# The low halves of the first MLP's weights, computed by GpSimd instead of VectorE

## The chip, the cores and the metric

The kernel runs on one core of a Trainium2 chip. The metric is the device time of one execution in microseconds, the median of the runs shown. The engines are TensorE (PE in the profile; its weight loads are PEld), VectorE (DVE), ScalarE (ACT), GpSimd (POOL) and SyncE (SP), which issues the transfers. Each works through its own instructions strictly in a fixed order, and semaphores hold an instruction until what it needs is there.

## The reference

An attention over windows of 32 queries, then two MLPs on its output, all in float32. The weights of the MLPs have their values in 8-byte cells when they come in, of which the kernel makes float32 again.

```python
def _attn_ref(q, k, v, mem_k, mem_v):            # q: 4 x 8 heads x 768 x 64
    for c in range(S // 32):                     # 16 keys of context left, 8 right, 8 memory keys
        k_full = np.concatenate([mem_k, k_ctx], axis=2)
        scores = scale * np.matmul(q_c, k_full.transpose(0, 1, 3, 2))
        a = softmax(scores)
        out[:, :, c_start:c_end] = np.matmul(a, v_full)

def _moe_ref(x, w_in, w_out):                    # x: 3072 x 512, w_in: 512 x 2048
    h = x @ w_in
    g = np.where(h > 0.0, h, np.exp(np.minimum(h, 0.0)) - 1.0)
    return g @ w_out

def _moe2_ref(x, w_in, w_out, s, b):             # same sizes
    r = np.maximum(x @ w_in, 0.0)
    return (s * (r * r) + b) @ w_out
```

## The kernel before

**Split matmuls.** TensorE multiplies in a reduced float32 format (F32R). To keep precision, each operand is split into a high half, the value rounded to that format, and a low half, the rest. A product is then three matmuls (`mm3`, L326 to L328): high by high, high weight by low data, low weight by high data. The third, L328, is the one that reads a weight's low half.

**The weights of the first MLP** are 32 slots: for each of 16 hidden chunks c, one slot of w_in (i = 0) and one of w_out (i = 1), 128 x 512 each. `load_w` (L125) brings a slot's 8-byte cells into a tile `raw`. `to_f32` takes them apart: two ScalarE conversions (L131, L132) and two VectorE merges (L135, L138) that leave the float32 value in a tile `t`, of which there are three buffers in turn (pool `wst`). Then `split_w` makes the halves: ScalarE writes the high one (L149), and L150 subtracts it from the value. In the profile L150's instruction stands at L184, the line of the helper `sub`, with the tile name w. `raw` and the finished pair share a place in memory, and every slot has a place of its own.

**The work beside it.** The attention goes by 24 units of 128 queries, each with scores (L219, psS or psVS), a softmax on VectorE and ScalarE (L228 to L237), transposes of the probabilities into `pt` (by TensorE, L251, for units 0 to 5; from unit 6 on by VectorE, L258) and values (L278, psV or psVS). From unit 6 on, one unit's values and the next one's scores share a pair of PSUM banks (`step_VS`). The tokens are 8 tiles of 384, three units each. For a tile t and a chunk c, `h1` does 12 matmuls into a bank psH (two such banks in turn, which the transposes of units 0 to 5 use too), then ScalarE (L350, L351) and VectorE (L352) make g in one buffer, and `split_g` its halves gh (ScalarE, L180) and gl (VectorE, L184). `out1` does 12 matmuls into four accumulators, two chunks behind `h1`. The sequence is tile 0 with chunks 0 to 5, tile 1 with all 16, tile 0 with the rest, then tiles 2 to 7. So each weight is made just before its first use for chunks 0 to 5 of tile 0, and some chunks ahead of it in tile 1. The second MLP follows with its own preparation, on which the change doesn't bear.

**What sets the order.** The program is written as steps in an order of priority (`weights_to` hands out weight steps beside attention and MLP steps); a scheduler then puts the instructions of each engine into one fixed row, by its own estimate of when each could start. A change of one instruction's engine can therefore move others.

Of the kernel before, what the change touches and what calls it, by code (L numbers as in the profile page):

```python
# [13 lines left out]
ALU = mybir.AluOpType  # L14
# [39 lines left out]
def tile_attention_then_two_mlps(ctx, tc, q_in, k_in, v_in, w1, w2, s_in, b_in, out):  # L54
# [17 lines left out]
    nc = tc.nc  # L72
# [43 lines left out]
    def f(t):  # L116
        return t.bitcast(F32)
# [10 lines left out]
    def to_f32(raw, t):  # L128

        low, high = raw[:, :, 0], raw[:, :, 1]  # L130
        nc.scalar.activation(out=f(high), in_=f(high), func=AF.Copy, scale=2.0 ** -112)  # L131
        nc.scalar.activation(out=low, in_=low.bitcast(U32), func=AF.Copy, scale=2.0 ** -29 * (1 - 2.0 ** -15),  # L132
                             bias=-0.4999)
        yield
        nc.vector.scalar_tensor_tensor(out=t, in0=high, scalar=3, in1=low,  # L135
                                       op0=ALU.logical_shift_left, op1=ALU.bitwise_or)
        yield
        nc.vector.scalar_tensor_tensor(out=t, in0=high, scalar=-0x80000000, in1=t,  # L138
                                       op0=ALU.bitwise_and, op1=ALU.bitwise_or)
        yield  # L140

    def split_w(c, i, raw):

        t = wst.tile([P, DM], I32, tag="t", name="t")
        yield from to_f32(raw, t)
        nm = "io"[i]
        parts = wps[c >= NFREE].tile([P, 2, DM], F32R, tag=f"w{i}_{c}", name=f"w{i}_{c}")
        hi, lo = parts[:, 0], parts[:, 1]
        nc.scalar.activation(out=hi, in_=f(t), func=AF.Copy)  # L149
        sub(lo, f(t), hi)  # L150
        W[nm, c], WT[nm, c] = (hi, lo), parts
        yield

# [8 lines left out]
    op = [actx.enter_context(tc.tile_pool(name="op", bufs=3))]  # L162
# [20 lines left out]
    def sub(lo, src, hi):  # L183
        return nc.vector.tensor_tensor(out=lo, in0=src, in1=f(hi), op=ALU.subtract)  # L184
# [310 lines left out]
    def weights_to(w, n, ahead):  # L495

        while wnext[0] < min(n, MICRO * NF):
            k, m = divmod(wnext[0], MICRO // 2)
            c, i = divmod(k, 2)
            load_ws(w, k + 1 + ahead)  # L500
            if m == 0:
                wsteps[:] = [split_w(c, i, wraw[k])]
            next(wsteps[0])
            wnext[0] += 1
# [297 lines left out]
```

## Time and profile before

| | |
|---|---|
| Median of 3 runs | 1099.0 us (1098.36 to 1099.37) |
| The profiled execution, its own time | 1097.48 us |
| Its span, first to last instruction | 1095.7 us |
| TensorE busy | 1076.3 us (98%), 8206 matmuls |
| VectorE busy | 783.9 us (72%), 1299 instructions |
| ScalarE busy | 591.9 us (54%), 939 instructions |
| GpSimd busy | 0.7 us, 6 instructions |

Busy times are of the profiled execution. Matmuls overlap in the pipeline, so that one of 384 columns is shown 336 ns long while the next starts some 0.17 us after it; a busy TensorE may still lose time between two. VectorE's instructions overlap a little too. The first 120 us, in which the weights of the first MLP are made, are a small part of the span; the shares above don't describe them.

### The profile page before, as it was taken

How to read it: one execution, taken by the hardware profiler on the slowest of the kernel's cores; microseconds unless marked ns; L12 is line 12 of the kernel's file. 1: busy time of each engine (PE TensorE's matmuls, PEld its weight loads, DVE VectorE, ACT ScalarE, POOL GpSimd, SP SyncE). 2: the span in 40 equal slices, each digit the busy share in tenths (PEclk: the TensorE clock that was granted, in tenths of full speed). 3: DMA queues.
4: the chain of work that ended last, by engine and by line, in shares of the span. 5: the costliest groups of instructions: out<-in, count | busy, mean ns of one | idle time of the engine just before them, and what ended most of it. 6: DMA issues, size and time to landing. Idle time of an engine off the chain costs nothing.

```text
span 1095.7 us, 20629 instructions
## 1 busy us (share of the span) xinstructions
PE 1076.3 (98%) x8206; PEld 964.4 (88%) x8206; DVE 783.9 (72%) x1299; ACT 591.9 (54%) x939; POOL 0.7 (0%) x6
## 2 busy tenths in 40 slices
PE   7999999999999999999999999999999999999998
PEld 5889999999999999999999987788888788888886
DVE  6899856777777777898884656796266695375844
ACT  4888534344344346887875455644355653355542
POOL 0000000000000000000000000000000000000000
PEclk7999999999999999999999999999999999999999
DMA  8965032442433316888876366777767777776773
GB/s 305 377 223 214 1 109 94 146 144 93 142 117 121 114 40 206 328 329 303 328 289 253 90 192 190 240 211 224 229 192 196 222 207 226 207 193 192 205 190 124
DMA packets 98113, 213.70 MB, mean 195 GB/s; under 512 B 9952, under 2 KB 27360, under 8 KB 95968
## 3 DMA queue, kind: packets, MB, share of 16 engines
q1 hardware_dynamic: 97440, 211.59, 60.3%
q8 instruction: 65, 1.06, 0.4%
q10 hardware_dynamic: 576, 0.79, 0.2%
q14 instruction: 32, 0.26, 0.1%
HBM read 164.89 MB, written 47.45 MB: 194 GB/s over the span
## 4 chain that ended last, share of the span: by engine, by line
PE 87%; DVE 6%; DMA 4%; ACT 3%; issue 1%; SPq 0%; ACTq 0%; DVEq 0%
PE psH L326 14%; PE psH L328 14%; PE psH L327 14%; PE psL L327 7%; PE psL L328 7%; PE acc L326 7%; PE psL L326 7%; PE acc L327 7%; PE acc L328 7%; DVE pt L258 2%; DMA xc<-y_dram 1%; PE psVS L278 1%; DMA xl<-x_dram 1%; PE psVS L219 1%; PE psV L278 1%
## 5 line engine op out<-in xcount | busy, mean ns | idle before, releaser
L326 PE MATMUL psH<-xh,w 128*128 128x384 f32 x512 | 174.9, 342 | 2.4 <-ACT pt L180 1.0
L326 PE MATMUL acc<-gh,w 128*128 128x384 f32 x512 | 172.7, 338 | 1.3 <-DVE big L380 0.8
L328 PE MATMUL psH<-xh,w 128*128 128x384 f32 x512 | 173.0, 338 | 0.0
L327 PE MATMUL psH<-xl,w 128*128 128x384 f32 x512 | 172.6, 337 | 0.2 <-DVE xl L184 0.2
L328 PE MATMUL acc<-gh,w 128*128 128x384 f32 x512 | 171.8, 336 | 0.0
L327 PE MATMUL acc<-gl,w 128*128 128x384 f32 x512 | 171.7, 335 | 0.0
L702 ACT ACTIVATE g2h<-g 128x1024 fp32r<-128x1024 f32 x84 | 88.9, 1058 | 95.6 <-PE psL L328 95.5
L327 PE MATMUL psL<-g2l,ws 128*128 128x512 f32 x336 | 133.0, 396 | 1.4 <-DVE g2l L184 1.4
L184 DVE TENSOR_TENSOR g2l<-g,g2h 128x1024 fp32r<-128x1024 f32 x84 | 102.3, 1222 | 44.3 <-ACT g2h L702 44.0
L328 PE MATMUL psL<-g2h,ws 128*128 128x512 f32 x336 | 132.9, 395 | 0.0
L326 PE MATMUL psL<-g2h,ws 128*128 128x512 f32 x336 | 132.5, 396 | 0.1
L326 PE MATMUL psH<-xc,ws 128*128 128x512 f32 x336 | 131.7, 397 | 0.5 <-ACT p L653 0.5
L327 PE MATMUL psH<-xc,ws 128*128 128x512 f32 x336 | 131.0, 390 | 0.0
L328 PE MATMUL psH<-xc,ws 128*128 128x512 f32 x336 | 131.0, 390 | 0.0
L350 ACT ACTIVATE g<-psH 128x384 f32<-128x384 f32 x128 | 62.5, 488 | 111.9 <-PE psH L328 65.3
L180 ACT ACTIVATE gh<-g 128x384 fp32r<-128x384 f32 x128 | 67.0, 523 | 88.0 <-DVE g L352 86.9
L352 DVE SCALAR_TENSOR_TENSOR g<-g,psH 128x384 f32<-128x384 f32 x128 | 70.4, 550 | 47.8 <-ACT g L351 46.9
L326 PEld LDWEIGHTS psH<-xh,w 128*128 128x128 f32 x512 | 96.7, 189 | 5.1 <-ACT pt L180 1.2
L326 PEld LDWEIGHTS acc<-gh,w 128*128 128x128 f32 x512 | 96.1, 188 | 2.8 <-DVE big L380 1.1
L327 PEld LDWEIGHTS psH<-xl,w 128*128 128x128 f32 x512 | 96.7, 189 | 0.5 <-DVE xl L184 0.4
L328 PEld LDWEIGHTS psH<-xh,w 128*128 128x128 f32 x512 | 96.7, 189 | 0.2
L327 PEld LDWEIGHTS acc<-gl,w 128*128 128x128 f32 x512 | 96.2, 188 | 0.1
(97 smaller groups left out, 1667.9 us busy)
## 6 DMA issues: line engine op xcount, KB each, us to landing
ws<-s_dram SPq DMA_DIRECT2D x336, 256.0 KB, 3.0
raw<-w SPq DMA_DIRECT2D x64, 512.0 KB, 5.5
s_dram<-right SPq DMA_DIRECT2D x16, 1024.0 KB, 4.6
kb<-k SPq DMA_DIRECT2D x24, 512.0 KB, 5.5
v<-v SPq DMA_DIRECT2D x24, 512.0 KB, 4.1
s_dram<-left SPq DMA_DIRECT2D x16, 768.0 KB, 3.6
q<-q SPq DMA_DIRECT2D x24, 256.0 KB, 5.4
out<-r SPq DMA_DIRECT2D x24, 256.0 KB, 3.5
```

The source lines that it names most:

```text
L180: return nc.scalar.activation(out=hi, in_=src, func=AF.Copy)
L184: return nc.vector.tensor_tensor(out=lo, in0=src, in1=f(hi), op=ALU.subtract)
L219: mm = nc.tensor.matmul(ps[o, z, r * NCK:(r + 1) * NCK], q[rows, r * U + c * CH:r * U + (c + 1) * CH], kb[rows, r, c * NCK:(c + 1) * NCK], ...
L258: nc.vector.transpose(out=pt[k * CH:(k + 1) * CH, :, rows], in_=sm[rows, :, z, n0:n0 + CH])
L278: nc.tensor.matmul(ps[r % 2 * D:(r % 2 + 1) * D, z, o:o + CH], v[rows, (r * NC + c) * D:(r * NC + c + 1) * D], pt[rows, r, cs], start=True ...
L326: nc.tensor.matmul(o, sa(a[0]), sb(b[0]), start=first, stop=False, skip_group_check=again)
L327: nc.tensor.matmul(o, sa(a[0]), sb(b[1]), start=False, stop=False, skip_group_check=again)
L328: return nc.tensor.matmul(o, sa(a[1]), sb(b[0]), start=False, stop=last, skip_group_check=again)
L350: nc.scalar.activation(out=g[:, :n], in_=ps[:, :n], func=AF.Relu, scale=-1.0)
L352: nc.vector.scalar_tensor_tensor(out=g[:, :n], in0=g[:, :n], scalar=-1.0, in1=ps[:, :n], op0=ALU.add, op1=ALU.max)
L702: nc.scalar.activation(out=gh, in_=g[:, block], func=AF.Copy)
```

## The change

One line of `split_w`: the subtraction is issued to GpSimd, with the same operands and the same result. In the profile it then has its own line, L150. The 32 instructions wait for ScalarE's high half; the merges that reuse a buffer `t` wait for GpSimd.

```diff
@@ split_w
         hi, lo = parts[:, 0], parts[:, 1]
         nc.scalar.activation(out=hi, in_=f(t), func=AF.Copy)
-        sub(lo, f(t), hi)
+        nc.gpsimd.tensor_tensor(out=lo, in0=f(t), in1=f(hi), op=ALU.subtract)
         W[nm, c], WT[nm, c] = (hi, lo), parts
```

The scheduler's rows move with it. VectorE before, around the weights of chunks 4 and 5 (t is the value, raw_c the cells of a slot of chunk c, w_c its halves, sm the probabilities, nmx their maxima):

```order
L138 SCALAR_TENSOR_TENSOR t<-raw_4_653,t 128x512
L228 TENSOR_TENSOR sm_103<-psS,cmask_92 128x2x4x64
L138 SCALAR_TENSOR_TENSOR t<-raw_5_713,t 128x512
L184 TENSOR_TENSOR w_4_853<-t,w_4_853 128x512
L231 TENSOR_REDUCE nmx<-sm_103 128x8
L184 TENSOR_TENSOR w_5_925<-t,w_5_925 128x512
L232 TENSOR_TENSOR sm_103<-sm_103,nmx 128x2x4x64
L352 SCALAR_TENSOR_TENSOR g<-g,psH 128x384
```

The same place of VectorE now:

```order
L228 TENSOR_TENSOR sm_103<-psS,cmask_92 128x2x4x64
L138 SCALAR_TENSOR_TENSOR t<-raw_5_713,t 128x512
L231 TENSOR_REDUCE nmx<-sm_103 128x8
L135 SCALAR_TENSOR_TENSOR t<-raw_5_744 128x512
L232 TENSOR_TENSOR sm_103<-sm_103,nmx 128x2x4x64
L138 SCALAR_TENSOR_TENSOR t<-raw_5_744,t 128x512
L352 SCALAR_TENSOR_TENSOR g<-g,psH 128x384
```

The two subtractions are gone, and the merges of the next slot stand in their place.

TensorE before, where chunk 5 of tile 0 begins (w_5_925 is chunk 5 of w_in):

```order
L278 MATMUL psV<-pt,v 64x32 x10
L326 MATMUL psH<-xh,w_5_925 128x384
L327 MATMUL psH<-xl,w_5_925 128x384
L278 MATMUL psV<-pt,v 64x32 x16
L328 MATMUL psH<-xh,w_5_925 128x384
```

TensorE there now:

```order
L328 MATMUL acc_760<-gh,w_3_751 128x384
L326 MATMUL psH<-xh,w_5_925 128x384
L327 MATMUL psH<-xl,w_5_925 128x384
L328 MATMUL psH<-xh,w_5_925 128x384
L326 MATMUL psH<-xh,w_5_925 128x384
```

The value matmuls between the second and the third matmul of the chunk went behind the chunk. At chunk 3 it is the same; at chunks 2 and 4 a unit's 32 score matmuls now stand in that gap.

TensorE before, after the last chunk of tile 0's first part, where unit 6's values and unit 7's first scores stand (psVS):

```order
L328 MATMUL acc_761<-gh,w_5_956 128x384
L278 MATMUL psVS<-pt,v 64x32 x32
L219 MATMUL psVS<-kb,q 32x64 x7
L326 MATMUL psH<-xh,w_2_592 128x384
L327 MATMUL psH<-xl,w_2_592 128x384
```

TensorE now, at the place of unit 7's values, 366 rows later, when unit 6's step has come 48 matmuls earlier:

```order
L328 MATMUL psH<-xh,w_9_1264 128x384
L278 MATMUL psVS<-pt,v 64x32 x9
L326 MATMUL acc_1996<-gh,w_7_1131 128x384
L327 MATMUL acc_1996<-gl,w_7_1131 128x384
L278 MATMUL psVS<-pt,v 64x32 x3
L328 MATMUL acc_1996<-gh,w_7_1131 128x384
L278 MATMUL psVS<-pt,v 64x32
L326 MATMUL acc_1997<-gh,w_7_1131 128x384
L327 MATMUL acc_1997<-gl,w_7_1131 128x384
L278 MATMUL psVS<-pt,v 64x32 x19
```

Unit 6's step no longer stands among the first chunks of tile 1 but behind all of them, 48 matmuls of the MLP ahead of unit 7's; between unit 7's and unit 8's steps stand 54 more after these rows, where before there were 60.

## Rows read from the trace of the kernel before

**Rows 1.** Stretches in us: busy us (instructions) by engine, granted clock, DMA share, GB/s

```profile
core 0: us, PE busy (x) PEld busy (x) DVE busy (x) ACT busy (x) POOL busy (x), PEclk, DMA share, GB/s
10.00:34.20 24.20, 18.40 (x418) 15.22 (x416) 19.05 (x38) 13.91 (x25) 0.00 (x0) 0.65 0.90 337
34.20:72.40 38.20, 36.41 (x484) 32.37 (x484) 37.43 (x75) 35.67 (x69) 0.00 (x0) 1.00 0.74 288
72.40:81.40 9.00, 7.46 (x121) 6.13 (x119) 8.80 (x20) 7.34 (x15) 0.00 (x0) 1.00 0.79 259
...
100.00:121.00 21.00, 21.00 (x122) 21.00 (x121) 20.68 (x38) 14.15 (x28) 0.00 (x0) 1.00 0.06 14
121.00:160.00 39.00, 39.00 (x343) 38.62 (x342) 22.18 (x51) 15.87 (x31) 0.00 (x0) 1.00 0.25 77
```

**Rows 2.** Tile w, subtractions: ns min/median/max, first and last start; then 34.2 to 72.4

```profile
L184 DVE TENSOR_TENSOR w<-t,w x32: 679/684/694, 16.4 to 120.3; 128x512 fp32r<-128x512 f32 x32
...
L184 DVE TENSOR_TENSOR w<-t,w x11: 679/684/693, 38.0 to 70.1; 128x512 fp32r<-128x512 f32 x11
```

**Rows 3.** Order of time, VectorE, 57 to 61 us: start, busy us, what

```profile
57.35 0.68 DVE L184 TENSOR_TENSOR w<-t,w 128x512 fp32r<-128x512 f32 x1
57.95 0.68 DVE L231 TENSOR_REDUCE nmx<-sm 128x8 f32<-128x512 f32 x1
58.55 0.68 DVE L184 TENSOR_TENSOR w<-t,w 128x512 fp32r<-128x512 f32 x1
...
59.75 0.55 DVE L352 SCALAR_TENSOR_TENSOR g<-g,psH 128x384 f32<-128x384 f32 x1
60.21 0.69 DVE L135 SCALAR_TENSOR_TENSOR t<-raw 128x512 int32<-128x512 int32 x1
```

**Rows 4.** Groups of GpSimd: busy us, mean ns | idle before

```profile
masks.py:199 POOL TENSOR_SCALAR_AFFINE_SELECT ident<-ident 128x128 f32<-128x128 f32 x1 | 0.3, 292 | 0.1
masks.py:197 POOL MEMSET ident<- 128x128 f32 x1 | 0.2, 205 | 0.3 <-POOLq L785 0.3
...
L785 POOL MEMSET const-float32-0.0<- 128x1 f32 x1 | 0.1, 98 | 0.2 <-issue 0.2
```

**Rows 5.** Groups of g and its halves, 0 to 420 us, columns as in rows 4

```profile
L184 DVE TENSOR_TENSOR gl<-g,gh 128x384 fp32r<-128x384 f32 x80 | 44.4, 556 | 20.2 <-ACT gh L180 19.5
L352 DVE SCALAR_TENSOR_TENSOR g<-g,psH 128x384 f32<-128x384 f32 x80 | 44.0, 551 | 33.6 <-ACT g L351 32.9
...
L351 ACT ACTIVATE g<-g 128x384 f32<-128x384 f32 x80 | 42.0, 524 | 2.0
L350 ACT ACTIVATE g<-psH 128x384 f32<-128x384 f32 x81 | 39.7, 490 | 86.8 <-PE psH L328 55.1 <-DVE gl L184 30.8 <-PE acc L328 0.8
```

**Rows 6.** Order of time, ScalarE and TensorE, 57 to 60 us, start of chunk 5

```profile
57.65 0.63 ACT L149 ACTIVATE w<-t 128x512 fp32r<-128x512 f32 x1
...
58.89 0.67 PE L278 MATMUL psV<-pt,v 64*64 64x32 f32 x32
59.49 0.44 PE L328 MATMUL psH<-xh,w 128*128 128x384 f32 x1
```

**Rows 7.** Order of time, TensorE, 72 to 76 us, with idle time and releaser

```profile
72.51 0.95 PE L278 MATMUL psVS<-pt,v 64*64 64x32 f32 x24
...
75.06 0.78 PE L278 MATMUL psVS<-pt,v 64*64 64x32 f32 x38 [0.36 <-DVE pt L258]
75.76 0.34 PE L219 MATMUL psVS<-kb,q 64*32 64x64 f32 x14
```

**Rows 8.** Order of time, TensorE and VectorE, 151 to 166 us, units 7 and 8

```profile
151.37 1.14 PE L278 MATMUL psVS<-pt,v 64*64 64x32 f32 x64
152.43 0.86 PE L219 MATMUL psVS<-kb,q 64*32 64x64 f32 x64
...
161.97 2.57 DVE L258 STREAM_TRANSPOSE pt<-sm 32x128 f32<-32x128 f32 x8
...
163.86 1.51 PE L278 MATMUL psVS<-pt,v 64*64 64x32 f32 x64
```

## The prediction

> **What bounds the kernel now.** I read first the table of stretches, to see which engine is full where the edited work lies, then the groups of the weight steps, then the order of time around the places where TensorE waits. TensorE is busy in nearly all of the span, so only time that it loses can move. Between 34.2 and 72.4 us, VectorE is busy 37.43 of 38.2 us and ScalarE 35.67, and TensorE loses a little all along; between 72.4 and 81.4 it is busy 7.46 of 9.0; from 100 to 121 it is full, with 122 matmuls in 21.00 us, 0.172 us each [rows 1]. All 32 subtractions lie between 16.4 and 120.3 us and hardly vary, 679 to 694 ns [rows 2]. After 121 us VectorE is half idle, and nothing of the change is there but the order of the attention. So two things are to be weighed: how much VectorE's queue holds TensorE up until 81 us, and what a slower subtraction on another engine does to those who wait for it.
>
> **What is taken from VectorE.** One subtraction is busy 684 ns, but the next instruction starts 0.60 us after it (57.35, 57.95, 58.55) [rows 2, 3]. 32 x 0.60 = 19.2 us leave its queue. 11 of them start between 34.2 and 72.4 us [rows 2], so 6.6 us there; later TensorE is full or nearly so. The gain isn't 6.6 us: ScalarE makes the high halves and all conversions, none of which is taken away, and is idle only 38.2 - 35.67 = 2.5 us of this stretch [rows 1]. With VectorE out of the way, TensorE could run at most some 2.5 us ahead, then ScalarE is late. Relief: -2.5 us at best.
>
> **What GpSimd's subtraction takes.** No row shows it. Its nearest rows are a memset of 1 column, 98 ns, one of 128 columns, 205, and a select that reads and writes 128 columns, 292 [rows 4]. By the memset's slope (0.82 ns a column) 512 columns take 0.52 us; by two passes at the select's (1.5 ns a column each) 1.64 us. I take 1.2 us, nearer the upper end, since it reads two operands. At one subtraction in 3.3 us (32 in 104 us) GpSimd itself keeps up by either end. (The Trainium skill, GPSIMD Engine Reference, section 3.1, states 4497 ns for a two-input operation on 2048 fp32 columns; an estimate from that for a quarter of the columns is 1.1 to 1.2 us, and the sum would stay as it is.)
>
> **What VectorE loses to it.** This decides the case. GpSimd's subtraction reads while VectorE works through its own two-operand instructions. Call x the time that one costs VectorE. The trace has no such pair: its six GpSimd instructions run in the first microseconds, beside memsets. From below, x = 0: VectorE's durations don't change (679 to 694 ns) though ScalarE and DMA are as busy as they can be [rows 1, 2]. From above, x is the whole 1.2 us, if VectorE stands still all along. Nothing here lies nearer to one end, so I take the middle, x = 0.6, and keep both. At x = 0.6 VectorE loses what it was spared, and the relief is nil. The point from which more is lost lies close by: in the steps of the second token tile (72 to 121 us) the new order puts two weight slots beside each hidden chunk. VectorE then has 0.46 + 0.46 us for g and its low half, of like length [rows 3, 5], 2 x (0.60 + 0.60) us for the two merges of each slot and 2 x, in all 3.32 + 2x; TensorE takes 24 x 0.172 = 4.13 us. x = 0.6 makes 4.52, 0.39 us late a step, 3.9 us in ten steps. TensorE has room for that: between the end of one psH and the next use of its bank lie 36 matmuls, 6.2 us, and the chain that frees the bank takes some 1.5 us (L350, L351 and L352, each about 0.5 us) [rows 5], so about 4.7 us are free. Cost there at x = 0.6: 0.
>
> **The latency of the low half.** TensorE's third matmul of a chunk (L328) needs it. For chunk 5 the high half ends at 57.65 + 0.63 = 58.28, VectorE's subtraction at 58.55 + 0.68 = 59.23, and L328 starts at 59.49; 16 value matmuls (x32 in the trace) stood ahead of it [rows 3, 6]. GpSimd ends at 58.28 + 1.2, and some 0.3 for the hand-over and a busy port: 0.5 us later. In the new order, chunks 2 and 4 have 32 score matmuls (some 0.8 us) between L327 and L328, which hides it, but chunks 3 and 5 have nothing. Where the high half is just in time, 1.1 us are lost; I count one of the two places: +1.0 us (both: 2.2; none, if ScalarE runs ahead: 0). From the second token tile on, the halves are made long before their use. Of the buffers t, three in number, each is held 0.5 us longer; L135 now waits for GpSimd to release one, and g's instructions stand behind it on VectorE. This is in x's upper end.
>
> **The attention step that moves.** Before, unit 6's values run at 72.51 us and wait for VectorE's transposes: 64 matmuls take until 75.76, 3.25 us, where the same work takes 1.06 at 151.37; 2.2 us lost [rows 7, 8]. In the new order this step stands over 350 rows later, so that loss goes. But then units 6, 7 and 8 follow each other closely, and one unit's chain is long: scores end at 153.29, the last transpose at 161.97 + 2.57 = 164.54, 11.3 us [rows 8]. Between units 6 and 7 there are now 53 matmuls of 0.172 and a few values, 10.0 us: 1.3 us of waiting. Between 7 and 8, 54 and a few values, 9.7 us: 1.6 us. Before it was 60, and the wait 0.4 us (1.51 instead of 1.14 us busy at 163.86) [rows 8]. Sum: -2.2 + 1.3 + 1.6 - 0.4 = +0.3 us. What is late next after 75.76 is VectorE's g, and that is in the first term.
>
> **Sum.** 0 (relief less x) + 0 (second tile) + 1.0 (latency) + 0.3 (attention) = +1.3 us. The profiled execution has a span of 1095.7 us and took 1097.48; the median of the runs is 1099.0, 1.5 us above it. I add the sum to the median: 1100.3 us.
>
> **Rivals.** *VectorE is relieved in full (x = 0).* For it: durations that don't react to other engines [rows 2]. Then -2.5 (relief) + 0.5 (latency, half as probable as weights come earlier) + 0.3 = -1.7, 1097.3 us. It reaches lower: ScalarE's idle time from 72.4 to 81.4, 1.66 us [rows 1], may go too, and the two waits behind the attention may be filled: 1095.5.
>
> *The two engines exclude each other (x about 0.8).* Slower, and it decides from x = 0.6 on. If an instruction with two operands in SBUF can't run beside GpSimd's reading, VectorE stands for the 1.2 us less what happens to run beside it. Of the 3.32 us that it works in a step, only the 0.46 of L352, which reads PSUM, don't collide. A third of the subtraction hidden so makes x = 0.8: 11 x 0.2 = 2.2 us late until 72 us; then 4.92 us a step, 7.9 in ten, 3.2 over the room; latency 1.5; attention 0.3. Sum +7.2, 1106 us. At x = 0.9 it would be 3.3 + 5.2 + 1.8 = +10.3, 1109. For it speaks that both merges of each slot and g's low half read two SBUF tiles, back to back; against it, that no row shows a collision. The Trainium skill (SBUF — State Buffer, "Who interferes with whom") states just this: a VectorE instruction with two SBUF inputs contends with a GpSimd instruction that reads SBUF, and the loser "**fully blocks**". By that rule the sum is this rival's, not mine; no run here shows it yet.
>
> *The change does nothing at all*: it moves instructions for certain, and TensorE loses time only before 81 us and in few waits later. 1099.0 lies inside the first case's bounds and gets no chance of its own.
>
> **How the numbers follow.** Chances: middle case 0.38, relief 0.32, exclusion 0.30. A measurement of this kernel can tell about 0.2%, 2.2 us, from no change, so the borders are 1096.8 and 1101.2. The middle case lies within by 0.22, above by 0.13 (two late chunks), below by 0.03; relief is below by 0.18, within by 0.13, above by 0.01; exclusion is above by 0.27, within by 0.03. Faster 0.21, same 0.38, slower 0.41. The range leaves out a tenth on each side: from 1095.5, the lower end of the relief, to 1107.5, past the exclusion at x = 0.8. The likeliest case's own range is 1098 to 1103.
>
> **What would show it.** The duration of GpSimd's subtraction (1.2 us) and the spacing of VectorE's merges beside it: 0.60 us still means x = 0; merges of over 1 us, or gaps before them, mean exclusion. VectorE's share between 34 and 72 us: some 82% with relief, near 98% in the middle case. TensorE waiting on GpSimd's w at chunks 3 and 5 for about a microsecond shows the latency; psVS waiting on pt twice after 140 us and not at 72, the attention term. I am wrong if TensorE's own losses until 81 us were not VectorE's doing, if its granted clock, 0.65 on the mean between 10 and 34 us and 1.00 after [rows 1], comes back at another time, or if the later order of transfers moves by more than the waits counted here.

## The result: slower, and by more than any case of the prediction

| | before | after |
|---|---|---|
| Median | 1099.18 us (4 runs, 1098.36 to 1099.44) | 1113.95 us (4 runs, 1113.18 to 1116.06) |
| Profiled execution, its span | 1097.48, 1095.7 us | 1116.06, 1114.3 us |

The ratio is 1.0138, 95% interval 1.0119 to 1.0157: 14.8 us slower by the medians. The prediction, 1100.3 us with a range of 1095.5 to 1107.5, is wrong. The profiled execution of after is the slowest of its four, and that of before took 1.7 us less than the median of before, so sums from the two traces run to 18.6 us, not 14.8.

The stretches of the profile after, in the columns of [rows 1]:

```profile
core 0: us, PE busy (x) PEld busy (x) DVE busy (x) ACT busy (x) POOL busy (x), PEclk, DMA share, GB/s
34.20:72.40 38.20, 32.20 (x450) 28.40 (x449) 36.46 (x54) 30.90 (x60) 14.47 (x11) 0.91 0.74 287
72.40:81.40 9.00, 8.24 (x48) 7.92 (x47) 8.75 (x23) 8.03 (x17) 2.73 (x3) 1.00 0.06 22
81.40:100.00 18.60, 14.27 (x74) 12.89 (x73) 18.57 (x23) 13.53 (x27) 10.98 (x9) 0.96 0.93 342
100.00:121.00 21.00, 20.24 (x108) 19.28 (x107) 18.48 (x24) 17.42 (x35) 9.56 (x7) 0.95 0.11 40
```

Two columns matter. VectorE is as full as before (36.46 of 38.2 us until 72, 18.57 of 18.6 until 100), but until 72 us it gets through 54 instructions instead of 75, and only 11 of the 21 missing ones are subtractions. And the granted clock, 1.00 in all of these stretches before, is 0.91, 0.96 and 0.95 in three of them.

What VectorE's instructions became is in the groups between 0 and 160 us (busy us, mean ns | idle before). First the two merges before:

```profile
L138 DVE SCALAR_TENSOR_TENSOR t<-raw,t 128x512 int32<-128x512 int32 x32 | 21.8, 684 | 0.1
...
L135 DVE SCALAR_TENSOR_TENSOR t<-raw 128x512 int32<-128x512 int32 x32 | 21.6, 682 | 0.4 <-ACT raw L132 0.3
```

Then the changed kernel (L150 is GpSimd's subtraction, with its shortest, median and longest in ns and its first and last start):

```profile
L150 POOL TENSOR_TENSOR w<-t,w x32: 1265/1424/1808, 15.0 to 126.7; 128x512 fp32r<-128x512 f32 x32
```

```profile
L138 DVE SCALAR_TENSOR_TENSOR t<-raw,t 128x512 int32<-128x512 int32 x32 | 29.3, 917 | 0.3
L135 DVE SCALAR_TENSOR_TENSOR t<-raw 128x512 int32<-128x512 int32 x32 | 29.2, 922 | 2.3 <-issue 1.7 <-ACT raw L132 0.6
L184 DVE TENSOR_TENSOR gl<-g,gh 128x384 fp32r<-128x384 f32 x24 | 16.3, 681 | 6.9 <-ACT gh L180 6.9
L352 DVE SCALAR_TENSOR_TENSOR g<-g,psH 128x384 f32<-128x384 f32 x24 | 13.1, 547 | 15.1 <-ACT g L351 15.1
...
L232 DVE TENSOR_TENSOR sm<-sm,nmx 128x512 f32<-128x512 f32 x3 | 4.2, 1413 | 0.0
...
L235 DVE TENSOR_SCALAR rs<-sums 128x8 f32<-128x8 f32 x8 | 2.7, 332 | 0.0
L231 DVE TENSOR_REDUCE nmx<-sm 128x8 f32<-128x512 f32 x3 | 2.0, 677 | 0.0
```

Both merges took 682 and 684 ns before and take 922 and 917; g's low half went from 556 [rows 5] to 681. L352, one of whose operands is in PSUM, stayed at 547 (551 in rows 5), and the reduction L231 at 677. All the lengthened instructions together (the merges 15.1 us, gl 3.0, L232 2.2, L235 1.3, the softmax product L237 1.1) make 22.7 us, or 0.71 us for each of GpSimd's 32 subtractions. VectorE was spared 19.2 us. So it ends 3.5 us worse off; that alone is not 15 us.

How one meeting looks is seen in order of time, VectorE and then GpSimd (start, busy us, what):

```profile
80.64 1.32 DVE L135 SCALAR_TENSOR_TENSOR t<-raw 128x512 int32<-128x512 int32 x1
81.89 1.62 DVE L184 TENSOR_TENSOR gl<-g,gh 128x384 fp32r<-128x384 f32 x1
83.43 0.68 DVE L138 SCALAR_TENSOR_TENSOR t<-raw,t 128x512 int32<-128x512 int32 x1
```

```profile
79.93 3.16 POOL L150 TENSOR_TENSOR w<-t,w 128x512 fp32r<-128x512 f32 x2 [6.28 <-ACT w L149]
```

GpSimd's two subtractions run from 79.93 to 83.09. In that time VectorE gets through one merge and most of one gl, which take 1.32 and 1.62 us; the next merge, at 83.43 with GpSimd idle, takes 0.68 again.

The whole trace shows what happens in a meeting. Of VectorE's 512- and 384-column instructions with two SBUF operands, 29 start while a subtraction of GpSimd's is running. All but two of them (which start as it ends) end at a fixed distance behind GpSimd's end: 0.55 us with 512 columns, 0.41 or 0.42 with 384, as the gl above (83.51 against 83.09). So they stand still until GpSimd is through, and nearly all of their work comes after it. The 14 that had started first keep their 0.54 to 0.69 us, and then it is GpSimd that waits: its subtraction takes 1.36 to 1.81 us if such an instruction is under way when it starts, and 1.27 to 1.31 otherwise. What VectorE loses in a meeting is thus about the rest of GpSimd's instruction.

### The profile page after: what moved, and what is told of

Same layout as the page of the kernel before. It is cut to its first block, busy times and chain, and to the rows that moved or that the text cites. A ratio compares the mean times of both kernels' runs of the same rounds, so it can differ in the third digit from the quotient of the medians.

```text
span 1114.3 us, 20683 instructions
## 1 busy us (share of the span) xinstructions
PE 1083.2 (97%) x8206; PEld 968.2 (87%) x8206; DVE 788.4 (71%) x1267; ACT 592.4 (53%) x939; POOL 46.8 (4%) x38
## 3 DMA queue, kind: packets, MB, share of 16 engines
q8 instruction: 65, 1.06, 0.4%
## 4 chain that ended last, share of the span: by engine, by line
PE 79%; DVE 9%; DMA 7%; ACT 2%; issue 2%; SPq 1%; POOL 0%; ACTq 0%; DVEq 0%; POOLq 0%
PE psH L326 13%; PE psH L328 13%; PE psH L327 13%; PE psL L327 7%; PE psL L328 7%; PE psL L326 6%; PE acc L326 6%; PE acc L328 6%; PE acc L327 6%; DVE pt L258 2%; DMA xc<-y_dram 2%; DMA xl<-x_dram 1%; DMA raw<-w 1%; PE psVS L278 1%; DMA x_dram<-xs 1%
## 5 line engine op out<-in xcount | busy, mean ns | idle before, releaser
L352 DVE SCALAR_TENSOR_TENSOR g<-g,psH 128x384 f32<-128x384 f32 x128 | 70.3, 549 | 49.3 <-ACT g L351 48.3
```

What stands on the lines that cost most here:

```text
L352: nc.vector.scalar_tensor_tensor(out=g[:, :n], in0=g[:, :n], scalar=-1.0, in1=ps[:, :n], op0=ALU.add, op1=ALU.max)
```

## The experiments

Each time is the median of four runs, or of ten where that is said. Beside it stands the ratio to the kernel before, run again on the same chip with the experiments (medians 1097.45 us for the first four, 1097.93 us for the last four).

To see where time is lost I also put the traces side by side by work done: TensorE's matmuls are summed up in order of time, each kind at the time that it takes without waiting (0.174 us for one of 384 columns, 1.07 us for 64 value matmuls, 0.79 for 64 score matmuls), and the table gives how much later than the kernel before (minus: earlier) a kernel reaches the same sum. As the orders differ, an entry holds to about 1 us, and less well beside a long wait (after at 88.2 lies on one: about 6.6 us ahead of it, 9.9 behind it).

| TensorE's lag in us, when before is at | 43.7 | 66.7 | 74.4 | 88.2 | 112.7 | 142.6 | 154.9 | 173.5 | end of span |
|---|---|---|---|---|---|---|---|---|---|
| after | 2.6 | 6.9 | 6.1 | 9.7 | 13.0 | 13.6 | 17.2 | 17.7 | 18.6 |
| e1, GpSimd only reads along | 0.9 | 4.8 | 7.2 | 8.4 | 12.6 | 15.2 | 15.0 | 15.7 | 13.8 |
| e3, GpSimd reads nothing | -0.4 | -3.4 | -5.3 | -5.6 | -6.1 | -5.8 | -1.8 | -1.3 | -1.3 |
| e7, GpSimd reads one operand | -0.5 | -2.6 | -3.2 | -2.7 | -3.2 | -2.9 | 3.3 | 4.0 | 1.4 |
| e4, late slots only | 0.8 | -0.1 | -1.4 | 5.5 | 13.9 | 14.2 | 16.7 | 17.7 | 18.3 |
| e5, early slots only | 1.5 | 4.4 | 3.5 | 2.8 | 3.0 | 3.4 | 6.9 | 7.4 | 6.2 |
| e6, half of each slot | 0.9 | 0.5 | -1.1 | 2.2 | 6.1 | 6.3 | 6.1 | 6.1 | 7.5 |
| e8, half relief, no reading | 2.2 | -0.3 | -1.2 | 1.2 | 1.2 | 1.3 | 1.3 | 1.2 | -0.5 |
| e9, high half on GpSimd | 0.8 | 0.8 | 1.8 | 2.6 | 2.1 | 2.5 | 5.0 | 6.4 | 5.1 |

**e1: the old kernel, with GpSimd reading along.** VectorE still makes the low halves; GpSimd then subtracts the finished halves, in four pieces of 128 columns, into a scratch tile that nobody uses. Nobody waits for GpSimd, and the rows of TensorE, VectorE, ScalarE and SyncE are in the old order.

```diff
         sub(lo, f(t), hi)
+        for k in range(KT):
+            cols = slice(k * P, (k + 1) * P)
+            nc.gpsimd.tensor_tensor(out=scr, in0=f(hi[:, cols]), in1=f(lo[:, cols]), op=ALU.subtract)
```

> The kernel before, with VectorE still making the low halves; GpSimd in addition makes 32 x 4 subtractions of 128 columns, of each slot's finished halves, into a scratch tile that nobody reads. The rows of TensorE, VectorE, ScalarE and SyncE are those of the kernel before. Theory A (VectorE's instructions with two operands in SBUF and GpSimd's reading exclude each other): nothing is taken from VectorE and some 20 us are added, merges and subtractions of 0.68 us reach 1 to 1.8 us, and the time rises by 15 to 25 us. Theory B (the new order costs the time): the order is the old one, so within 1 us of before. Theory C (the low half comes later and holds the buffers t): nobody waits for GpSimd here, so within 1 us of before.

Measured: 1111.04 us, ratio 1.0112 (1.0095 to 1.0128): 13.6 us slower. The groups of VectorE and GpSimd, 0 to 170 us (in this kernel L188 is the subtraction and L356 is g):

```profile
L135 DVE SCALAR_TENSOR_TENSOR t<-raw 128x512 int32<-128x512 int32 x32 | 26.3, 833 | 0.0
L138 DVE SCALAR_TENSOR_TENSOR t<-raw,t 128x512 int32<-128x512 int32 x32 | 25.9, 812 | 0.1
L188 DVE TENSOR_TENSOR w<-t,w 128x512 fp32r<-128x512 f32 x32 | 25.5, 803 | 0.0
L188 DVE TENSOR_TENSOR gl<-g,gh 128x384 fp32r<-128x384 f32 x26 | 18.4, 709 | 3.4 <-ACT gh L184 3.4
L356 DVE SCALAR_TENSOR_TENSOR g<-g,psH 128x384 f32<-128x384 f32 x26 | 14.2, 547 | 10.5 <-ACT g L355 10.5
```

```profile
L153 POOL TENSOR_TENSOR scr<-w 128x128 f32<-128x128 f32 x128 | 89.1, 696 | 54.1 <-DVE w L188 45.0
```

The same instructions are lengthened, by some 18 us in all, and L356 with its PSUM operand again isn't. GpSimd's reading alone, without a new order and without a later low half, makes a loss nearly as large as the change's. It isn't the same dose, though: GpSimd is busy for 89 us here, not 46, and VectorE is relieved of nothing.

**e3: the new kernel, with GpSimd reading nothing.** GpSimd writes zeros where it would subtract; the rows of VectorE, ScalarE and SyncE are those of the changed kernel.

```diff
-        nc.gpsimd.tensor_tensor(out=lo, in0=f(t), in1=f(hi), op=ALU.subtract)
+        nc.gpsimd.memset(f(lo), 0.0)
```

> The changed kernel, with GpSimd writing zeros into the low halves instead of subtracting, so it reads nothing and the products lose their third term. The rows of VectorE, ScalarE and SyncE are those of the changed kernel. A: merges are back at 0.68 us each, VectorE is relieved by 19 us, and the time is 1095 to 1099.5 us, as the prediction's case of full relief has it. B: the order is unchanged, so the loss stays, over 1108 us. C: the zeros come some 0.8 us sooner than the differences did, so most of the loss goes, as with A.

Measured: 1096.69 us (10 runs), ratio 0.9991 (0.9975 to 1.0008). The whole loss is gone: between this kernel and the changed one, in the same order, lie some 16 us by their ratios, and they are GpSimd's reading (a subtraction of 1.44 us in the mean instead of a memset of 0.53, and what it holds up). The table tells more than the time. With VectorE relieved, TensorE is some 6 us ahead from 88 to 143 us; then it loses 4.0 us within one attention step. The values of units 7 and 8 in this kernel:

```profile
147.77 0.41 PE L278 MATMUL psVS<-pt,v 64*64 64x32 f32 x10
148.47 0.31 PE L278 MATMUL psVS<-pt,v 64*64 64x32 f32 x6 [0.28 <-DVE pt L258]
149.11 0.30 PE L278 MATMUL psVS<-pt,v 64*64 64x32 f32 x2 [0.33 <-DVE pt L258]
...
151.28 0.78 PE L278 MATMUL psVS<-pt,v 64*64 64x32 f32 x38
151.99 0.86 PE L219 MATMUL psVS<-kb,q 64*32 64x64 f32 x64
...
162.53 0.92 PE L278 MATMUL psVS<-pt,v 64*64 64x32 f32 x26
163.81 0.78 PE L278 MATMUL psVS<-pt,v 64*64 64x32 f32 x38 [0.36 <-DVE pt L258]
164.52 0.86 PE L219 MATMUL psVS<-kb,q 64*32 64x64 f32 x64
```

Unit 7's 64 value matmuls take from 147.77 to 151.99, 4.22 us instead of the 1.06 that they need: 3.2 us of waiting for the transposes, spread over small gaps of which the profile names only some. Unit 8's take 1.99: 0.9 us. In the changed kernel the same two places read 165.94 to 170.16 and 180.69 to 182.68, the same 3.2 and 0.9 us. Since one kernel comes there 5.8 us early and the other over 13 us late, this cost belongs to the order. VectorE's row in the changed kernel shows where it comes from:

```profile
162.50 0.56 DVE L380 COPY big<-acc 128x384 f32<-128x384 f32 x1 [1.55 <-DMA y_dram<-big]
...
165.31 3.87 DVE L258 STREAM_TRANSPOSE pt<-sm 32x128 f32<-32x128 f32 x12
```

At the new place two copies of the second tile's accumulators (L380) stand in unit 7's softmax chain, and the second waits 1.55 us, ahead of all the transposes, for the transfer that frees its buffer. From the last score matmul (155.74) to the end of the last transpose (169.18) the chain takes 13.4 us, with 10.2 us until the values start: 3.2 us of waiting.

**e7: GpSimd reads one operand.** It copies the value into the low half, which then isn't the low half.

```diff
-        nc.gpsimd.tensor_tensor(out=lo, in0=f(t), in1=f(hi), op=ALU.subtract)
+        nc.gpsimd.tensor_copy(lo, f(t))
```

> The changed kernel, with GpSimd copying the value into the low half: one operand read instead of two, so the low halves are wrong. Same rows of VectorE, ScalarE and SyncE. A: if any reading by GpSimd excludes VectorE's second operand, VectorE loses in proportion to the copy's shorter time, 1100 to 1108 us; if only two-operand reading does, 1095 to 1099.5. B: over 1108 us. C: between the zeroing and the subtraction.

Measured: 1100.0 us (10 runs), ratio 1.0018 (1.0004 to 1.0031), 3.3 us over e3. Groups, 0 to 170 us:

```profile
L135 DVE SCALAR_TENSOR_TENSOR t<-raw 128x512 int32<-128x512 int32 x32 | 24.3, 768 | 3.4 <-ACT raw L132 2.5 <-issue 0.6
L138 DVE SCALAR_TENSOR_TENSOR t<-raw,t 128x512 int32<-128x512 int32 x32 | 22.9, 719 | 0.3
```

```profile
L150 POOL CAST w<-t 128x512 fp32r<-128x512 f32 x32 | 24.6, 770 | 82.2 <-DVE t L138 62.2 <-ACT g L350 4.9 <-ACT g L351 4.2
```

The merges are still held up, by 0.08 and 0.03 us in the mean against e3. The copy takes half as long as the subtraction, and costs VectorE 0.14 us (4.6 us in all: 3.8 of the merges, 0.8 of gl and L237) where the subtraction costs 0.71. The meeting is of the same kind: a merge that starts beside a copy ends 0.54 us after it, and takes up to 1.10 us. There is only less left of a copy (0.61 us at its shortest) to wait for.

**e4: only the late slots.** GpSimd makes the low halves of chunks 6 to 15 (20 slots), which are needed long after they are made; VectorE makes those of chunks 0 to 5.

```diff
+        if c < HF:
+            sub(lo, f(t), hi)
+        else:
-        nc.gpsimd.tensor_tensor(out=lo, in0=f(t), in1=f(hi), op=ALU.subtract)
+            nc.gpsimd.tensor_tensor(out=lo, in0=f(t), in1=f(hi), op=ALU.subtract)
```

> GpSimd makes the low halves of chunks 6 to 15 only (20 slots, from about 66 us on), VectorE those of chunks 0 to 5, which are made just before their use. A: the loss that the trace shows after 70 us stays, about 5 to 8 us, 1104 to 1107. B: part of the order moves back; no firm number, 1099 to 1114. C: these halves are made some 10 us ahead of their use, so nothing is lost, 1098 to 1100.

Measured: 1114.27 us, ratio 1.0138 (1.0116 to 1.016): as much as all 32 slots, and two to three times the 5 to 8 us that theory A had given; it lies just outside the ranges of B and C too. Until 74 us this kernel runs like the one before; then it loses 15 us in 38. The stretch of six steps from one g to the next, before, in the columns of [rows 1]:

```profile
75.64:102.43 26.79, 26.65 (x218) 25.08 (x211) 26.43 (x47) 25.23 (x50) 0.00 (x0) 1.00 0.80 293
```

VectorE and GpSimd in the same six steps of this kernel, 76.71 to 115.80 us:

```profile
L135 DVE SCALAR_TENSOR_TENSOR t<-raw 128x512 int32<-128x512 int32 x15 | 16.9, 1147 | 1.2 <-POOL w L153 1.2
L138 DVE SCALAR_TENSOR_TENSOR t<-raw,t 128x512 int32<-128x512 int32 x16 | 13.4, 854 | 0.1
L187 DVE TENSOR_TENSOR gl<-g,gh 128x384 fp32r<-128x384 f32 x6 | 6.5, 1085 | 0.0
```

```profile
L153 POOL TENSOR_TENSOR w<-t,w 128x512 fp32r<-128x512 f32 x15 | 24.0, 1617 | 20.8 <-ACT w L149 20.8
```

A step is 39.1 / 6 = 6.5 us long instead of 4.5. VectorE was full there before (26.43 of 26.79 us), so each microsecond that a merge or gl is held up shows in the step. The excess is 15 x 0.46 + 16 x 0.17 + 6 x 0.53 = 12.8 us, 0.86 for each of 15 subtractions. Fifteen of them fell into the six steps, 2.5 a step and not 2: in this kernel's row of VectorE they stand closer together there (15 merges L135, 12 in the six steps before). A late low half at the urgent chunks 3 and 5 can have no part in it, since this kernel leaves those to VectorE.

**e5: only the early slots.** The mirror of e4: GpSimd makes chunks 0 to 5, VectorE the rest, with TensorE's order all but that of the changed kernel.

```diff
+        if c >= HF:
+            sub(lo, f(t), hi)
+        else:
-        nc.gpsimd.tensor_tensor(out=lo, in0=f(t), in1=f(hi), op=ALU.subtract)
+            nc.gpsimd.tensor_tensor(out=lo, in0=f(t), in1=f(hi), op=ALU.subtract)
```

> GpSimd makes the low halves of chunks 0 to 5 (12 slots, nearly all before 72 us), VectorE those of chunks 6 to 15; the attention stands as in the changed kernel. The late slots alone cost as much as all 32 (1114.3 us). Theory A (a GpSimd subtraction holds VectorE's two-operand instructions up wherever VectorE has no idle time, and the loss adds up): TensorE is 6 to 7 us behind at 72 us as in the changed kernel, cannot catch up in the second tile, where it is full, and the moved attention step costs its 4 us (2.7 come back by 220 us): 1103 to 1106 us. Theory D (what is lost early is given back while VectorE has slack later, and the second tile alone counts): 1097 to 1100 us.

Measured: 1104.2 us, ratio 1.0066 (1.0048 to 1.0084), inside what exclusion gives and 4 us above the other theory. What is lost before 72 us is not given back while TensorE is full: the lag is 3.5 us at 74 us and 3.0 at 113. At units 7 and 8, 3.5 us are added (3.4 to 6.9), as in the kernels of the same order. Theory A's time came out right in part by luck, for two of its steps are wrong and cancel: the lag at 74 us is 3.5 us and not 6 to 7 as in the changed kernel, and no 2.7 us come back by 220 us, in this kernel or in the changed one.

**e6: half of each slot.** GpSimd subtracts 256 columns, VectorE the other 256. The attention of unit 6 stands where it stood before.

```diff
-        nc.gpsimd.tensor_tensor(out=lo, in0=f(t), in1=f(hi), op=ALU.subtract)
+        h = DM // 2
+        nc.gpsimd.tensor_tensor(out=lo[:, :h], in0=f(t)[:, :h], in1=f(hi[:, :h]), op=ALU.subtract)
+        sub(lo[:, h:], f(t)[:, h:], hi[:, h:])
```

> Each low half is shared: GpSimd the first 256 columns, VectorE the other 256; the attention step of unit 6 stands at its old place in TensorE's order. Theory A: GpSimd reads for about half as long, so some 10 us of holding-up instead of 19.4 (changed kernel against the one without reading, at 142 us), less about 3 us of relief, and no loss from the attention: 1102 to 1106 us, a long VectorE instruction again whenever GpSimd runs beside it. Against A: if what costs is a fixed price for each meeting and not the length of the reading, the loss stays near 19, less 3: 1111 to 1114.

Measured: 1102.33 us, ratio 1.0049 (1.0031 to 1.0066). It is the length of the reading that costs, not the number of subtractions, of which there are 32 here too. The two halves of the subtraction, 0 to 170 us:

```profile
L186 DVE TENSOR_TENSOR w<-t,w 128x256 fp32r<-128x256 f32 x32 | 20.9, 656 | 0.8 <-ACT w L149 0.7
```

```profile
L151 POOL TENSOR_TENSOR w<-t,w 128x256 fp32r<-128x256 f32 x32 | 29.1, 912 | 89.9 <-ACT w L149 86.3 <-DMA raw<-w 3.6
```

The two halves wait for the same ScalarE instruction and so run side by side: VectorE's takes 656 ns, the same instruction 422 in e8, where GpSimd reads nothing. Over all instructions it is 0.36 us for each half, half of 0.71. The loss shrinks by more: 5.8 us lie between this kernel and e8, against some 16 between the changed kernel and e3.

**e8: half the relief, nothing read.** As e6, but GpSimd writes zeros into the second 256 columns.

```diff
-        nc.gpsimd.tensor_tensor(out=lo, in0=f(t), in1=f(hi), op=ALU.subtract)
+        h = 256
+        nc.gpsimd.memset(f(lo[:, h:]), 0.0)
+        sub(lo[:, :h], f(t)[:, :h], hi[:, :h])
```

> VectorE subtracts only the first 256 columns of each low half, GpSimd writes zeros into the other 256 without reading anything (so the result is not the reference's); the attention step of unit 6 stands at its old place. It tells what the moved attention step costs. Theory P (the new place, 50 instructions ahead of the next unit, costs about 4 us): half the relief, about 3 us, stays to the end, no lag appears around unit 7 and 8: 1093.5 to 1095.5 us, below the kernel with all 512 columns zeroed (1096.7). Theory Q (whoever runs ahead by some microseconds waits there, wherever the step stands): the 3 us are lost around units 7 and 8: 1096.5 to 1098 us.

Measured: 1096.55 us (10 runs), ratio 0.9991 (0.9979 to 1.0003). By the time alone theory Q would be right, by the trace neither is. No lag appears at unit 7 (1.3 us at 142.6 and at 154.9), as P says; the same holds for e1 and e6, which have the old place too, while every kernel with values or scores moved to some 50 rows ahead of unit 7's loses time there: after, e3, e4, e5 and e9 2.5 to 4 us, e7 6.2, of which up to 3.4 belong to a low clock (granted 0.50 from 151.7 to 158.5 us of its trace). But the 3 us of relief that P wanted to keep don't last that long: at 74 us this kernel is 1.2 us ahead, at 88 us 1.2 behind. Unit 6's values stand there, at their old place:

```profile
72.23 0.62 PE L280 MATMUL psVS<-pt,v 64*64 64x32 f32 x24
73.19 0.30 PE L280 MATMUL psVS<-pt,v 64*64 64x32 f32 x2 [0.34 <-DVE pt L260]
74.44 0.67 PE L280 MATMUL psVS<-pt,v 64*64 64x32 f32 x32 [0.95 <-DVE pt L260]
75.62 0.69 PE L328 MATMUL psH<-xh,w 128*128 128x384 f32 x1 [0.52 <-DVE g L354]
76.11 0.52 PE L329 MATMUL psH<-xl,w 128*128 128x384 f32 x1
76.43 0.52 PE L330 MATMUL psH<-xh,w 128*128 128x384 f32 x1
```

They wait for VectorE's transposes, but no longer than before [rows 7]. New are 0.52 us of waiting for g, and matmuls that then follow each other every 0.32 us instead of 0.17 until 78.67 us, at a granted clock of 0.50; in the kernel before, the clock stayed at 1.00 behind the same place. Nine matmuls at the lower clock are some 1.4 us, the larger part of the 2.4. So in this order it is more the clock than the attention that took the relief, in the one execution that was traced; the ten runs reach from 1094.42 to 1100.73 us. That was a third outcome which I had not listed.

**e9: the high half on GpSimd.** The kernel before, with ScalarE's rounding copy given to GpSimd.

```diff
-        nc.scalar.activation(out=hi, in_=f(t), func=AF.Copy)
+        nc.gpsimd.tensor_copy(hi, f(t))
         sub(lo, f(t), hi)
```

> The other way round: the kernel before, with the rounding copy that makes the high half (one operand read) moved from ScalarE to GpSimd; VectorE keeps its subtraction. It tells whether ScalarE is the next bound, as the prediction's limit of the relief said, and whether one-operand reading is cheap here too. ScalarE is spared some 16 us; VectorE loses about 0.14 us a copy, 4.5 us, as in the run where GpSimd copied. If VectorE alone sets TensorE's losses until 81 us: 1098 to 1103 us. If ScalarE holds TensorE up as much: 1093 to 1097 us.

Measured: 1101.85 us, ratio 1.0042 (1.0026 to 1.0058). Relieving ScalarE, by 15 us between 34 and 121 us (60.28 us busy instead of 75.76), brings nothing that outweighs what the copies cost VectorE (merges L135 807 ns instead of 682, gl 596): ScalarE doesn't hold TensorE up as much as VectorE does. What a relief of ScalarE alone would bring was not run. The kernel is 2.5 us behind at 143 us, up to 1.7 of it by a low clock (0.50 from 77.5 to 80.9 us), and loses as much again at unit 7. VectorE's subtraction now waits for GpSimd's copy, and TensorE too (1.5 us in three waits for L149).

No version that computes everything beat the kernel before. The two that leave the reading out are equal to it within the interval, so even a relief for nothing would be worth at most 2.7 us, by the interval of e3, with these orders of the attention.

## Why the prediction was wrong

**What VectorE loses (x): the right question, the wrong case.** I set x between 0 and 1.2, took 0.6 and gave exclusion 0.30. Measured are 0.71 us in the mean and 0.86 where VectorE is full. The mechanism is that of the exclusion rival, with the mark that was named for it: merges of over 1 us next to GpSimd's subtraction. VectorE's 95% until 72 us tells nothing apart, since the middle case had named 98%. The Trainium skill (SBUF — State Buffer, "Who interferes with whom") states that a VectorE instruction with two SBUF inputs contends with a GpSimd instruction that reads SBUF, and the trace agrees: the two-operand instructions are held up for the rest of GpSimd's, 1.32 and 1.62 us instead of 0.68 and 0.55, L352 with one operand in PSUM isn't (547 ns), and GpSimd, whose subtraction takes 1265 ns at its shortest, is stretched to 1808. I had written that nothing lay nearer to one end; for a rule that speaks against the change and fits the very operands, a middle value was the wrong default. That 0.6 lies near the mean of 0.71 is luck, for it was the middle between two ends and no account of a meeting. And x isn't what makes the miss: with 0.71 my sum would have come to about +4 us (1.2 + 1.4 + 1.2 + 0.3), with 0.86 to about +9. What failed is what the sum made of x in the two tiles.

**GpSimd's own time** was taken as 1.2 us and is 1.27 at its shortest, 1.42 at the median. This step held.

**The room in the second tile: the step that failed, together with the first tile.** At x = 0.6 this term was 0, and exclusion got 4.7 us off, for the room between a psH bank's last and next use. There was none of it left. TensorE was already waiting for g ahead of the second tile, and waits for it again within it (after, start, busy us, [idle before and releaser]):

```profile
64.57 0.69 PE L326 MATMUL psH<-xh,w 128*128 128x384 f32 x1 [2.42 <-DVE g L352]
65.05 0.53 PE L327 MATMUL psH<-xl,w 128*128 128x384 f32 x1
65.37 0.53 PE L328 MATMUL psH<-xh,w 128*128 128x384 f32 x1
...
97.69 0.45 PE L326 MATMUL psH<-xh,w 128*128 128x384 f32 x1 [2.27 <-DVE g L352]
```

The room was worked out from TensorE's side and from the length of g's chain. But g stands in VectorE's row behind the merges, VectorE was full in these steps before (8.80 of 9.0 us [rows 1], 26.43 of 26.79 in six steps), and so g comes later by all that VectorE loses. Between 74 and 113 us the changed kernel loses 6.9 us more (6.1 to 13.0), where my exclusion case had 3.2 over its room and the middle case none.

**The first tile.** Relief less x was to be 0, and 2.2 us in the exclusion case; the changed kernel is 6.1 us behind at 74 us. With the same order, e3 is 5.3 us ahead there: 11.4 us for some 14 subtractions. They met not only the merges: in 34.2 to 72.4 us two softmax differences L232 took 1774 ns each and three tiny L235, 8 columns, 629 instead of 160. These lie on the attention's chain, which I hadn't counted. A part of the 6.1 us is the clock, as follows.

**The clock** was in the last sentence of the prediction, as a thing that would make it wrong, but in no term. The rows above show it: after the idle 2.42 us the matmuls follow each other every 0.32 us instead of 0.17, which is the lower of TensorE's two levels, 1.2 instead of 2.4 GHz. The granted clock is 0.50 in three stretches of the trace: 50.8 to 54.2 us, 64.5 to 67.9 and 98.6 to 102.0, each behind a wait of 1.4 us or more (1.44 at 49.21, 2.42 at 64.57, 2.27 at 97.69). From 34.2 to 121 us the two kernels compare so (before, then after, columns as in rows 1):

```profile
34.20:121.00 86.80, 83.46 (x858) 77.42 (x859) 85.22 (x162) 75.76 (x147) 0.00 (x0) 1.00 0.60 224
```

```profile
34.20:121.00 86.80, 74.94 (x674) 68.49 (x673) 82.25 (x121) 69.88 (x136) 37.74 (x26) 0.94 0.56 211
```

TensorE stands idle 8.5 us longer (83.46 less 74.94), and a mean clock of 0.94 takes up to 0.06 x 86.8 = 5.2 us more. Together they make at most 13.7 us, where the lag grows by some 11 in this stretch. So up to 5.2 us of its loss are the clock, two thirds of them in the first tile. The low clock doesn't follow from the waits alone: e5 has waits of 1.46 us at 47.66 and of 2.44 at 62.50, like the first two above, and its clock is 1.00 all along. Its lag at 74 us is 3.5 us, not 6.1.

**Relief.** I said 2.5 us at best, then ScalarE is late. e3 gains 5.8 us (at 143 us). 2.2 of these are the wait at unit 6, which I had counted in the attention term; the other 3.6 are above 2.5, and near the 4.2 that ScalarE's idle time makes with the 1.66 us from 72 to 81. That ScalarE set this limit is not shown.

**The latency of the low half** was the largest term of the likeliest case, +1.0 us. TensorE waits once for GpSimd's low half, for 0.3 us:

```profile
PE psH L326 <- DVE g L352: 7.0, 7, 2.4
...
PE psH L328 <- POOL w L150: 0.3, 1, 0.3
```

These are TensorE's waits in all of the execution (us in total, times, longest); before, the first of them was 0.5 us, once. The hand-over, put at some 0.3 us with a busy port, was 0.08 us: so long after the end of ScalarE's high half GpSimd starts, in 28 of the 32 slots. The wait had been looked for at the wrong engine.

**The attention step** was named rightly and sized too low: the wait at unit 6 is gone (unit 6's values take 1.06 us at 153.82), and there are waits at units 7 and 8. But they are 3.2 and 0.9 us, not 1.3 and 1.6, so with the 2.2 gained and 0.4 no longer lost the term is +1.5, not +0.3. TensorE's work between the units 6 and 7 was right (10.2 us, 10.0 predicted), the chain was not: I took its 11.3 us over from the old place, and at the new one it is 13.4, with the accumulators' copies in it and the transfer that the second of them waits for. In e3 GpSimd reads nothing and the waits are the same, so it isn't contention.

**The sum, by the table:** in the profiled execution -5.8 (relief, with unit 6's wait: e3 at 142.6), +19.4 (reading, with the clock that is low in the changed kernel and not in e3: from there to 13.6), +4.1 (units 7 and 8, to 17.7) and +0.9 later make 18.6 us. e4, with 20 late slots alone, loses more in its six steps (39.1 us instead of 26.8) than the changed kernel in its own, which take 32.7 us, from 79.10 to 111.81. VectorE's row accounts for that: 31 merges stand in e4's six steps, 25 in the changed kernel's, 23 before. Six merges more at 0.60 us are 3.6 us, and the lengthening is 12.8 us in e4 and some 9.5 in the changed kernel (merges of 1060 and 964 ns, gl of 770, beside 12 subtractions). The changed kernel has the other merges earlier, and lost its 6.1 us there.

What stays open is the clock: no run has the changed kernel's order, its reading and a full clock, so the clock's part is known only as an upper bound, and why it fell here and not in e5 is not shown.

## What to carry to other kernels

An instruction is not free on an idle engine if it reads two SBUF operands while VectorE is full of instructions that do so too: each such instruction of VectorE's that starts beside it waits for the rest of GpSimd's, here 0.71 to 0.86 us for each subtraction, which is more than the 0.60 that was saved. Neighbours that read PSUM or reduce were not held up in these traces, and a GpSimd instruction that only writes held nobody up. Slack that was worked out for a wait counts only if the instruction that ends it isn't queued behind the lengthened ones, and only if nothing used it up before. What a relief is worth is read at the next wait behind it: in the new order one step of the attention took back 4 of 5.8 us.

## What was not expected of the hardware

- GpSimd's subtraction of 128 columns took 696 ns in the mean beside VectorE (e1), four of them twice as long as one of 512 columns (1446 ns). In small pieces the same reading still holds VectorE's instructions up by some 18 us, against 22.7.
- An instruction of 8 columns and one SBUF tensor (L235, 160 ns alone) took up to 1.26 us beside a subtraction; so not only instructions with two SBUF tensors are held up. Copies from PSUM, reductions and 32 x 32 transposes kept their times (L380 548 ns, L231 677).
- GpSimd's writing alone costs VectorE nothing that shows: beside 32 memsets of 527 ns (e3) the merges take 685 and 688 ns.
